# The first loads of a fused attention and gated feed-forward kernel, split over two queues, and the norm's gains loaded as rows

## The chip, the cores and the metric

The kernel runs on one core of a Trainium2 chip. The metric is device microseconds of one execution; the time of a kernel is the median of its runs. The profile is one execution of its own, recorded by the hardware profiler.

## The reference

Linear attention without a softmax, normed per head, and then a feed-forward layer with a sigmoid gate:

```python
# q, k, v: (8, 8, 576, 64) fp32; g_norm: (64,)
kv  = einsum('bhsd,bhse->bhde', k, v)
out = einsum('bhsd,bhde->bhse', q, kv)
out = out / sqrt(mean(out * out, -1) + 1e-6) * g_norm
x   = out.transpose(0, 2, 1, 3).reshape(4608, 512)
y   = (sigmoid(x @ w_gate) * (x @ w_val)) @ w_out   # w_gate, w_val: 512x1536, w_out: 1536x512
```

The weights come as 64-bit floats, 8 bytes an element, and the kernel turns them into 32-bit floats itself, with integer and float steps on VectorE and ScalarE.

## The kernel before

The rows of x are worked on in nine chunks of 512. Chunk 0 goes through both weight layers with plain products; the later chunks use a fast matrix scheme with fewer products (lines 1037 and 1139), which is most of the time and which the change does not touch. Attention of batch 0 is done in the head of the program, in four pairs of heads; attention of the later batches is fed in between the products of the chunks.

The order of the work is written out by hand: a manual schedule is used, and each engine executes its instructions in the order in which the code emits them. For the head that order is a string of tokens, `order`. `KV0`, `KVO0`, `Q0`, `QO0`, `U0`, `SQ0`, `SUM0`, `ROOT0`, `NORM0`, `X0`, `XO0` are the steps of pair 0: the product of k and v on TensorE (L346) and its copy by VectorE (L350), the turn of q by TensorE (L356) and its copy by ScalarE (L361), the output product (L373), its squares (ScalarE, L378), their sum (VectorE, L382), root (ScalarE, L386), the norm (VectorE, L390 and L392), the turn of the normed rows by TensorE (L400) and their copy to xT (ScalarE, L409). `warm10` is ten products of the identity with itself (L727), whose result nobody reads; they stand where TensorE would otherwise wait. `g0.0` to `g0.4` and `v0.0` to `v0.4` are the five steps of the conversion of a gate and a value block (L212, L230, L242, L247, L254), `ag` and `av` their steps on ScalarE (L217, L235), and `b0.0.0` and so on are products of chunk 0 (L666). The beginning reads:

```python
w1 w2 warm10 KV0 warm4 Q0 KVO0 QO0 warm3 U0 KV1 KVO1 Q1 SQ0 QO1 SUM0 ROOT0 g0.0 warm4 U1 NORM0 SQ1 ...
```

Ahead of these tokens the loads are emitted: `load_kv(n)` loads k and v of pair n (L97, 288 KB each), `load_q(n)` loads q of the pair in two halves, one for each head (L104, 144 KB each), and `load_unit(0, ...)` the gate block and then the value block of the first 64-bit weight unit (L163, 512 KB each). All of these are issued by SyncE. `g_norm` is loaded by ScalarE into `g_col`, one column of 128 partitions, in two transfers of 64 elements (L321); then ScalarE loads its table with a first square root (L325). `g_col` is read in the last conversion step of every gate and value block (L254). The identity is made by GpSimd (masks.py:197 and 199); GpSimd's queue has no transfer before the late q loads (L122).

A transfer issued by SyncE or ScalarE signals the end of its landing on one of eight semaphores, which are handed out in turn. The issue of a transfer waits until the last user of its semaphore has landed, so at most eight of these transfers are under way, and an issue that waits holds all that follows it on its engine. GpSimd's transfers have eight semaphores of their own.

Of the kernel before, what the change touches and what calls it, by code (L numbers as in the profile page):

```python
# [10 lines left out]
FP32 = mybir.dt.float32  # L11
# [10 lines left out]
def kernel(  # L22
# [11 lines left out]
    nc = tc.nc  # L34

    B, H, S, HD = q.shape
    T, DM = out.shape
    DF = moe_w_gate.shape[1]
    P = 128
    NHP = H // 2  # L40
    NJ = 6
# [10 lines left out]
    QB = 32  # L52
    NAT = 3
    NC = HD // QB
# [8 lines left out]
    NMT = DM // P  # L63
# [10 lines left out]
    RIGHT, LEFT, MIDDLE = 480, 128, 288  # L74
    const = ctx.enter_context(tc.tile_pool(name="const", bufs=1))
# [10 lines left out]


    NE = NHP
    pairs = {n: {} for n in range(B * NHP)}

    def load_kv(n):
        if n >= NE:
            return
        b, h0 = n // NHP, 2 * (n % NHP)
        for name, src in (("k", k), ("v", v)):
            t = first.tile([NP, 2, NJ * HD], FP32, tag=name, name=name)
            nc.sync.dma_start(out=t, in_=src[b, h0:h0 + 2].rearrange("h (p j) d -> p h (j d)", j=NJ))  # L97
            pairs[n][name] = t

    def load_q(n):  # L100
        h0 = 2 * n
        t = first.tile([NP, NJ, 2, HD], FP32, tag="q", name="q")
        for e in range(2):
            nc.sync.dma_start(out=t[:, :, e, :], in_=q[0, h0 + e].rearrange("(p j) d -> p j d", j=NJ))  # L104
        pairs[n]["q"] = t

    q_late = {}
# [45 lines left out]
    def load_unit(u, halves=(0, 1)):  # L153
        if u >= len(units):
            return
        kind, f = units[u]
        if 0 in halves:
            staged[u] = raw.tile([P, 2, DM], I64, tag="st", name="st", bufs=NST)
        st = staged[u]
        for i in halves:  # L160
            if kind == "gv":
                src = (moe_w_gate, moe_w_val)[i].rearrange("(m p) f -> p m f", p=P)[:, :, P * f:P * f + P]
                nc.sync.dma_start(out=st[:, i].rearrange("p (m f) -> p m f", m=NMT), in_=src)  # L163
            else:
                nc.sync.dma_start(out=st[:, i], in_=moe_w_out[P * (f + i):P * (f + i) + P, :])

# [27 lines left out]
    def convert(u):  # L194
# [42 lines left out]
        def s2(some=slice(None)):  # L237

            m = d["m"]
            if u > 2:  # L240
                load_unit(u - 1 + NST, (1,))
            vec.scalar_tensor_tensor(out=m[:, some], in0=words(u)[0][:, some], scalar=2.0 ** -52, in1=m[:, some],  # L242
                                     op0=ALU.mult, op1=ALU.add)
# [6 lines left out]
        def s4(some=slice(None)):  # L250

            m, p = d["m"][:, some], d["p"].bitcast(FP32)[:, some]
            if kind == "gv":
                vec.scalar_tensor_tensor(out=m, in0=m, scalar=g_col, in1=p, op0=ALU.mult, op1=ALU.mult)  # L254
            else:
                vec.tensor_tensor(out=m, in0=m, in1=p, op=ALU.mult)
            if u > 1 and some.stop != NMT:
                load_unit(u + NST, (0,))
# [36 lines left out]
            elif u + 1 in BY_SCALAR:  # L295
                conversion[u + 1]["ahead"][i - 2]()

    for n in range(4):
        load_kv(n)
        load_q(n)  # L300
        if n in (1, 2):
            load_unit(0, (n - 1,))


    eps = const.tile([P, 1], FP32, name="eps")
    g_col = const.tile([P, 1], FP32, name="g_col")
    unused = const.tile([P, 1], FP32, name="unused")
    const.tile([P, LEFT // 4], FP32, name="low_pad")
    w1 = const.tile([P, N3, 4 * NMT, 2, P], FP32, name="w1")
    w2 = const.tile([P, NFT, DM], FP32, name="w2")  # L310
    ident = const.tile([P, P], FP32, name="ident")
# [5 lines left out]
    qTs = const.tile([P, QW], FP32, name="qTs")  # L317
    sqs = const.tile([P, 2 * NU * P], FP32, name="sqs")
    xTs = const.tile([P, NC, 2, S // 2], FP32, name="xTs")
    for e in range(2):  # L320
        nc.scalar.dma_start(out=g_col[HD * e:HD * e + HD], in_=g_norm.rearrange("(d o) -> d o", o=1))  # L321
    make_identity(nc, ident)
    nc.vector.memset(eps, 1e-6)

    nc.scalar.activation(out=unused, in_=eps, func=AF.Sqrt)  # L325


    NX = 3
# [271 lines left out]
    def store(c, t, ot, cols=slice(0, DM), queues=(nc.sync,)):  # L600

        r0 = i = 0
        while r0 < P:
            b, s = divmod(G * c + P * t + r0, S)
            rows = out[S * b:S * b + S, cols]
            if b < NE // NHP:
                j, p = divmod(s, NP)
# [42 lines left out]
    def early(n):  # L650

        def ps(kind):
            if kind == "kv":
                return pair_kv.unsqueeze(1)
            return psum0.tile([P, 2, 512], FP32, tag="q" if kind == "q" else f"ux{n % 2}", name="two")
        return ps
# [34 lines left out]
    KV, KV_OUT, Q, Q_OUT, U, U_SQUARE, U_SUM, U_ROOT, U_NORM, X, X_OUT = range(11)  # L691
    a = [attention(n, early(n)) for n in range(NE)]

# [14 lines left out]
    for token in order.split():  # L708
        name = token.rstrip("0123456789.")
        n = [int(i) for i in token[len(name):].split(".")]  # L710
        f = n[0]
        if name == "b":
            if f not in blks:
                if f:
                    two = early(NE)("q")
                blks[f] = Plain(0, F_ORDER[f], (two[:, 0], two[:, 1]) if f else (warm, pair_kv))
            blks[f].mm(n[1], n[2])
        elif name in ("G", "E"):
            (blks[f].gate if name == "G" else blks[f].end)()
        elif name in ("g", "v", "ag", "av"):  # L720
            m0 = NMT * (name[-1] == "v")
            conversion[f]["a" if name[0] == "a" else "c"][n[1]](slice(m0, m0 + NMT))
        elif name == "w":
            load_unit(f)
        elif name in ("warm", "warmk"):
            for _ in range(f):
                nc.tensor.matmul((warm if name == "warm" else pair_kv)[:, 0:P], ident, ident, start=True, stop=True)  # L727
        else:
            a[f][steps[name]]()
            if token == f"Q{NE - 1}":  # L730
                first_ctx.__exit__(None, None, None)
                hp = ctx.enter_context(tc.tile_pool(name="hp", bufs=1))
                h_main = [hp.tile([P, 4 * NT, P], FP32, name=f"h{j}") for j in range(N3)]
                h_more = hp.tile([P, N3, 3 * NT, P], FP32, name="h_more")
# [159 lines left out]
    for some in places.split():  # L894
        p, names = some.split(":")
# [372 lines left out]
```

## Time and profile before

| | us |
|---|---|
| runs | 997.12, 997.27, 997.98; median 997.27 |
| profiled execution, its time | 996.52 |
| profiled execution, span of the trace | 994.7 |
| TensorE (PE) busy | 989.4 |
| VectorE (DVE) busy | 715.0 |
| GpSimd (POOL) busy | 614.1 |
| ScalarE (ACT) busy | 349.1 |

The span goes from the first to the last instruction in the trace; the execution's own time is 1.8 us longer. In the views, PE is TensorE's product, PEld its weight load, SPq, ACTq and POOLq are the sequencers of SyncE, ScalarE and GpSimd, whose DMA issues are not counted as busy time. A product of 32-bit floats takes several passes, so one product is two rows in the trace at most places (20 rows for ten warming products). The ends of TensorE's rows are modelled.

### The profile page before, as it was taken

Reading aid. Unit: us, or ns where it says so; the run is one execution under the profiler, and the core shown is the slowest. Engines: PE = TensorE matmul, PEld = TensorE weight load, DVE = VectorE, ACT = ScalarE, POOL = GpSimd, SP = SyncE. Lnnn points to the kernel's source line nnn. Section 1 sums busy time; section 2 is a strip of 40 time slices with the busy share of each in tenths; the row PEclk is TensorE's granted clock in tenths of the full one; section 3 lists DMA queues with packets and bytes.
Section 4 is the critical chain, followed back from the end, with each engine's and each line's share of the span. In section 5 each row is a group of like instructions: output and inputs, shape, how many; then the busy total and the mean of one; then the engine's idle time right before and its main releaser. Section 6 shows DMA issues by size and latency. Waiting matters only on the chain.

```text
span 994.7 us, 16605 instructions
## 1 busy us (share of the span) xinstructions
PE 989.4 (99%) x5958; PEld 814.9 (82%) x5958; DVE 715.0 (72%) x1199; ACT 349.1 (35%) x631; POOL 614.1 (62%) x991
## 2 busy tenths in 40 slices
PE   9999999999999999999999999999999999999998
PEld 7454448888888888888888888888888888888887
DVE  5999997898768666785777576866686566756672
ACT  5577523661244213530344124412442133213320
POOL 1349996798169625864386717870786359734963
PEclk9999999999999999999999999999999999999999
DMA  9986507662889568746975677656854455545514
GB/s 275 291 239 219 166 28 210 193 236 89 277 278 282 170 190 275 197 151 195 271 225 162 204 224 248 184 163 210 280 165 156 139 198 190 165 141 172 214 48 123
DMA packets 149523, 194.97 MB, mean 196 GB/s; under 512 B 79840, under 2 KB 121696, under 8 KB 149440
## 3 DMA queue, kind: packets, MB, share of 16 engines
q0 software_dynamic: 22512, 116.41, 35.3%
q1 hardware_dynamic: 120848, 75.66, 26.5%
q10 hardware_dynamic: 6080, 1.84, 0.8%
q8 instruction: 47, 0.77, 0.3%
q14 instruction: 36, 0.29, 0.1%
HBM read 160.04 MB, written 25.56 MB: 187 GB/s over the span
## 4 chain that ended last, share of the span: by engine, by line
PE 99%; ACT 0%; POOL 0%; issue 0%; DVE 0%; POOLq 0%; ACTq 0%
PE mm L1037 54%; PE mm L1139 27%; PE mm L666 7%; PE mm L913 4%; PE at L497 2%; PE mm L727 1%; PE at L447 1%; PE two L666 1%; PE at L666 1%; PE mm L447 1%; PE mm L346 0%; PE two L373 0%; PE two L356 0%; PE at L436 0%; PE two L400 0%; ACT qTs L361 0%
## 5 line engine op out<-in xcount | busy, mean ns | idle before, releaser
L1037 PE MATMUL mm<-xs,w 128*128 128x256 f32 x1428 | 331.3, 379 | 0.0
L1037 PEld LDWEIGHTS mm<-xs,w 128*128 128x128 f32 x1428 | 270.9, 190 | 37.0
L1037 PE MATMUL mm<-xT,w 128*128 128x256 f32 x948 | 230.5, 380 | 0.0
L1037 PEld LDWEIGHTS mm<-xT,w 128*128 128x128 f32 x948 | 179.6, 190 | 25.0 <-issue 0.5
L855 POOL DMA_DIRECT2D w<-kept x84 | 46.9, 559 | 203.1 <-PE mm L1037 199.6
L1007 DVE TENSOR_TENSOR sg<-sg,mm 128x512 f32<-128x512 f32 (+1 forms) x176 | 100.8, 600 | 89.8 <-PE mm L1037 34.3
L1139 PE MATMUL mm<-w,h 128*128 128x256 f32 x630 | 142.9, 379 | 0.0
L1139 PEld LDWEIGHTS mm<-w,h 128*128 128x128 f32 x630 | 119.6, 190 | 16.4 <-POOL h L999 0.2
L1003 ACT COPY temps<-mm 128x512 f32<-128x512 f32 (+1 forms) x128 | 66.0, 537 | 187.1 <-PE mm L1139 94.7
L999 POOL TENSOR_TENSOR h<-h,sg 128x512 f32<-128x512 f32 x72 | 96.6, 1360 | 46.0 <-ACT sg L996 30.2
L808 POOL TENSOR_TENSOR h<-h 128x128 f32<-128x128 f32 x216 | 110.5, 524 | 16.5 <-DVE h_more L808 13.1
L1139 PE MATMUL mm<-w,h_more 128*128 128x256 f32 x474 | 108.2, 379 | 0.0
L996 ACT ACTIVATE sg<-sg 128x512 f32<-128x512 f32 x96 | 59.7, 630 | 127.3 <-DVE sg L1007 127.3
L1139 PEld LDWEIGHTS mm<-w,h_more 128*128 128x128 f32 x474 | 90.1, 190 | 12.2
L1003 ACT COPY sg<-mm 128x512 f32<-128x512 f32 (+1 forms) x112 | 57.1, 510 | 87.5 <-PE mm L1139 45.3
L808 POOL TENSOR_TENSOR h_more<-h 128x128 f32<-128x128 f32 x120 | 58.6, 492 | 34.6 <-DVE h L999 30.3
L1007 DVE TENSOR_TENSOR temps<-temps,mm 128x512 f32<-128x512 f32 (+1 forms) x96 | 59.5, 620 | 26.6 <-PE mm L1139 16.9
L1007 DVE TENSOR_TENSOR temps<-mm,temps 128x512 f32<-128x512 f32 (+1 forms) x64 | 39.9, 623 | 53.3 <-PE mm L1139 23.9
L1003 ACT COPY h<-mm 128x512 f32<-128x512 f32 x48 | 28.1, 585 | 129.9 <-PE mm L1037 116.4
L666 PE MATMUL mm<-xT,w 128*128 128x512 f32 x160 | 70.1, 595 | 0.0
L1007 DVE TENSOR_TENSOR sg<-mm,sg 128x512 f32<-128x512 f32 (+1 forms) x64 | 39.7, 620 | 41.8 <-PE mm L1139 21.9
L808 POOL TENSOR_TENSOR h<-h,h_more 128x128 f32<-128x128 f32 x120 | 60.9, 508 | 4.6
(164 smaller groups left out, 1273.9 us busy)
## 6 DMA issues: line engine op xcount, KB each, us to landing
w<-kept POOLq DMA_DIRECT2D x42, 896.0 KB, 5.4
w<-kept POOLq DMA_DIRECT2D x90, 384.0 KB, 4.3
w<-kept POOLq DMA_DIRECT2D x42, 768.0 KB, 5.0
out_dram<-sg SPq DMA_DIRECT2D x119, 64.0 KB, 1.7
q<-in_q_dram SPq DMA_DIRECT2D x96, 72.0 KB, 5.0
xT<-xTs SPq DMA_DIRECT2D x96, 72.0 KB, 4.4
st<-in_moe_w_gate_dram SPq DMA_DIRECT2D x12, 512.0 KB, 6.2
st<-in_moe_w_val_dram SPq DMA_DIRECT2D x12, 512.0 KB, 6.4
```

The costliest lines, as they stand in the source:

```text
L447: nc.tensor.matmul(ps[m][HD * g:HD * g + HD, e], mains[2 * m + g, "k"][:, c], mains[2 * m + g, "v"][:, c], start=(b == 2 and e == 0 and j ...
L497: nc.tensor.matmul(to[HD * e:HD * e + HD], qTs[HD * g:HD * g + HD, c:c + HD], kvq[HD * g:HD * g + HD, m, e], start=True, stop=True)
L666: nc.tensor.matmul(self.ps[i], w[("wg", "wv")[i], self.f][:, m, :], xT[self.c][:, m, :], start=(m == 0), stop=(m == NMT - 1), skip_group_c ...
L808: ops.append((eng, lambda v=v, x=x, sign=sign, y=y, eng=eng: eng.tensor_tensor(out=h_form(v, j), in0=h_form(x, j), in1=h_form(y, j), op=op ...
L855: nc.gpsimd.dma_start(out=granule(g)[:, 0:n], in_=kept1[g // NPA % N3, g % NPA][:, 0:n])
L913: nc.tensor.matmul(ps[t], gv[0, f][:, P * t:P * t + P], w["wo", f], start=(f == 0), stop=(f == NFT - 1), skip_group_check=True)
L996: nc.scalar.activation(out=o["o" + step[1]], in_=o["o" + step[1]], func=AF.Sigmoid)
L999: mult.tensor_tensor(out=o[x], in0=o[x], in1=o[y], op=ALU.mult)
L1003: nc.scalar.copy(out=o[out_], in_=o[expr])
L1007: tt(out=o[out_], in0=o[x], in1=o[y], op=ALU.add if sign == "+" else ALU.subtract)
L1037: nc.tensor.matmul(regions[name][1][:, g], ws[:, g], xf[c][wv], start=(new and g == 0), stop=True, skip_group_check=True)
L1139: nc.tensor.matmul(regions[name][1], h_form(hv, j), ws[:, j], start=(used[i] and j == 0), stop=(j == N3 - 1), skip_group_check=True)
```

## The change

- The loads of pair 0 stay ahead of the constants; the loads of pairs 1 to 3 and the first gate and value block are emitted after them, in the same order among themselves.
- v of pairs 0, 1 and 2, the second half of q of pairs 0 and 1, and the second half of the first gate block (which becomes two transfers of 256 KB) are issued by ScalarE. On ScalarE, the first two of them stand ahead of the table load, and the other four behind the first square root.
- `g_norm` is loaded by GpSimd as four rows of 32 elements, each into the first row of a block of 32 partitions of `g_rows` (a part of `xTs` that is not yet in use, cleared by VectorE before). After the token `KVO0` VectorE turns `g_rows`, block by block of 32 by 32, into `g_turned`, whose first column is the new `g_col`.
- The string `order` is the same. The instructions of TensorE are the same in number, kind and order.

On the two queues the first transfers then stand in this order, with the landing that an issue waits for in brackets:

```
SyncE:   k0, first half of q0, k1, first half of q1, first half of the gate block, k2 [k0],
         first half of q2 [first half of q0], second half of q2 [first half of q1],
         value block [v1], k3 [first half of the gate block], v3 [second half of q1], q3 ...
ScalarE: v0, second half of q0, (table load, square root), v1, second half of q1 [v0],
         second half of the gate block [second half of q0], v2 [k1], then the copy of q of pair 0
GpSimd:  identity, four rows of g_norm
```

```diff
     def load_kv(n):
...
+            queue = nc.scalar if name == "v" and n < NTWO + 1 else nc.sync
-            nc.sync.dma_start(out=t, in_=src[b, h0:h0 + 2].rearrange("h (p j) d -> p h (j d)", j=NJ))
+            queue.dma_start(out=t, in_=src[b, h0:h0 + 2].rearrange("h (p j) d -> p h (j d)", j=NJ))
...
     def load_q(n):
...
+            queue = nc.scalar if e == 1 and n < NTWO else nc.sync
-            nc.sync.dma_start(out=t[:, :, e, :], in_=q[0, h0 + e].rearrange("(p j) d -> p j d", j=NJ))
+            queue.dma_start(out=t[:, :, e, :], in_=q[0, h0 + e].rearrange("(p j) d -> p j d", j=NJ))
...
+                if u == 0 and i == 0:
+                    for m, queue in ((0, nc.sync), (NMT // 2, nc.scalar)):
+                        queue.dma_start(out=st[:, i].rearrange("p (m f) -> p m f", m=NMT)[:, m:m + NMT // 2],
+                                        in_=src[:, m:m + NMT // 2])
+                else:
...
-    for n in range(4):
-        load_kv(n)
-        load_q(n)
-        if n in (1, 2):
-            load_unit(0, (n - 1,))
+    load_kv(0)
+    load_q(0)
...
-    g_col = const.tile([P, 1], FP32, name="g_col")
+    g_turned = const.tile([P, LEFT // 4], FP32, name="g_turned")
+    g_col = g_turned[:, 0:1]
...
-    for e in range(2):
-        nc.scalar.dma_start(out=g_col[HD * e:HD * e + HD], in_=g_norm.rearrange("(d o) -> d o", o=1))
+    g_rows = xTs[:, 0, 0, 0:QB]
+    nc.vector.memset(g_rows, 0.0)
     make_identity(nc, ident)
+    for n in range(P // QB):
+        nc.gpsimd.dma_start(out=g_rows[QB * n:QB * n + 1], in_=g_norm.rearrange("(o i d) -> o i d", o=1, d=QB)[:, n % NC])
     nc.vector.memset(eps, 1e-6)
...
     nc.scalar.activation(out=unused, in_=eps, func=AF.Sqrt)
+    for n in range(1, 4):
+        load_kv(n)
+        load_q(n)
+        if n < 3:
+            load_unit(0, (n - 1,))
...
+            if token == "KVO0":
+                nc.vector.transpose(g_turned[:, 0:QB], g_rows)
```

(`NTWO` is 2, `QB` 32, `P` 128, `NMT` 4, `NC` 2, `HD` 64.)

## The prediction

> **What bounds the kernel now.** I read the chain of waits of the first 24 us first, because every edit of the diff lies there, then the busy time by stretch, then the timelines of the queues that the edits touch. In the chain the columns are start, length, and what held the end.
>
> ```profile
> 1.02 0.30 POOL ident masks.py:199
> 1.32 0.04 issue
> 1.37 4.46 PE mm L727 x20
> 5.82 0.85 PE mm L346 x24
> 6.67 1.09 PE mm L727 x8
> 7.76 0.50 PE two L356 x6
> 8.26 0.70 PE mm L727 x6
> 8.95 0.03 issue
> 8.99 0.81 PE two L373 x40
> 9.80 0.85 PE mm L346 x24
> ...
> 21.84 0.65 ACT qTs L361
> ```
>
> The chain runs on TensorE from the moment the identity exists (1.37 us), and no DMA stands in it: L727 are the warming multiplications, L346, L356 and L373 the k-v, q and output products of a pair. TensorE by stretch says the same:
>
> ```profile
> 1.40:6.00 4.60, 4.60 (x28) 4.48 (x30) 0.00 (x0) 1.49 (x2) 0.00 (x0) 1.00 0.84 237
> 6.00:12.00 6.00, 5.97 (x122) 5.57 (x118) 1.45 (x4) 2.01 (x4) 0.00 (x0) 1.00 1.10 297
> 18.00:24.00 6.00, 5.94 (x101) 3.73 (x92) 5.56 (x13) 4.35 (x10) 1.94 (x3) 1.00 1.04 323
> ```
>
> The first number behind the comma is busy TensorE: 4.60 of 4.60, 5.97 of 6.00, 5.94 of 6.00 us; from 36 to 990 us it is busy throughout. The last two columns, DMA share and GB/s, say that the transfers already fill the DMA engines (shares near and over 1) at 237 to 323 GB/s. So the loads are busy, but TensorE does not wait for them: the warming multiplications fill the time until data land. That is what decides this case, since the change leaves TensorE's instructions and their order as they are, warming ones included.
>
> **SyncE.** The transfers below move in part to ScalarE:
>
> ```profile
> 0.74 0.38 SPq L97 DMA_DIRECT2D k<-in_k_dram  x1
> 1.18 0.44 SPq L97 DMA_DIRECT2D v<-in_v_dram  x1
> 1.66 1.40 SPq L104 DMA_DIRECT2D q<-in_q_dram  x2
> 3.10 0.62 SPq L97 DMA_DIRECT2D k<-in_k_dram  x1
> 3.76 0.45 SPq L97 DMA_DIRECT2D v<-in_v_dram  x1
> 4.26 1.24 SPq L104 DMA_DIRECT2D q<-in_q_dram  x2
> ```
>
> SyncE loses v of pairs 0 to 2 (0.44, 0.45, 0.67 us of issue), the second half of q of pairs 0 and 1 (about 0.7 and 0.63) and half a gate load. Its k of pair 1 then goes out at about 0.74 + 0.38 + 0.73 + gaps = 2.0 us instead of 3.10. What could TensorE gain? Its first k-v product waits for k and v of pair 0: v landed 3.6 us after its issue, at 4.8 us, while the product starts at 5.75, when ten warming multiplications are through. The second half of q lands 4.5 us after 2.43, at 6.9; its product starts at 7.60. Both had 0.7 to 0.9 us to spare, so earlier landings buy nothing. All that is not TensorE in the chain between 1.37 and 36 us is 0.65 (the q copy above) and some 0.15 of issue, 0.8 us together, and it waits for engines, not loads; 0.8 us is the bound of the gain, and I take 0.
>
> [...]
>
> The late loads: v of pair 3 lands at about 19.5 (issued 11.98, landing 7.6 us later, the longest of the v rows), its product starts at 20.19. After the change k of pair 3 is issued behind the landing of half a gate load (the semaphore that it shares) instead of q of pair 1. The whole gate load lands 6.2 us after 5.55, at 11.7, so k may go out up to 1.2 us later than its 10.52. At that moment k, v and q of pair 2 and the value load, 1376 KB, are still queued, 4.8 us at 290 GB/s: the engines do not run dry, and the bytes ahead of pair 3 are the same. Cost 0; if the cover failed, up to 1.2 - 0.65 = 0.6 us.
>
> **ScalarE.** It loses two g_col issues and gets six transfers: v and half a q of pair 0, then behind the table load v, half a q, half a gate load and v of pair 2. Before:
>
> ```profile
> 0.75 1.21 ACTq L321 DMA_DIRECT2D g_col<-in_g_norm_dram  x2
> 2.00 1.28 ACT L325 ACT_TABLE_LOAD   x1 [2.00 <-issue]
> 3.29 0.20 ACT L325 ACTIVATE unused<-eps 128x1 f32<-128x1 f32 x1
> 8.29 0.64 ACT L361 COPY qTs<-two 128x576 f32<-128x576 f32 x1 [4.80 <-PE two L356]
> ```
>
> The first two cost 0.44 + 0.7 = 1.1 us in place of 1.21, so the table load stays at 2.0. The last four cost about 0.45 + 0.63 + 0.62 + 0.67 = 2.4 us, under the 4.80 us that ScalarE is idle. But three of them wait for landings: half of q of pair 1 for v of pair 0, half the gate load for half of q of pair 0, and v of pair 2 for k of pair 1. Queued behind that last one is the copy of q at 8.29, and for that copy waits TensorE's output product at 8.99 (three warming multiplications fill only up to about 8.8). In the trace k of pair 1 landed 4.8 us after 3.10, at 7.9. With the same landing, v of pair 2 is issued from 7.9 to 8.6 (0.67 us) and the copy is 0.3 us late; with the longest issue of a row, 1.39 us (k of pair 2), to 9.3, 1.0 us late. But k of pair 1 is now third in its queue, issued 1.1 us earlier, with 288 KB less ahead of it on that queue: at a landing before 7.6 us nothing is late. Bounds 0 and 1.0; I take 0 to 0.3, as fewer bytes stand ahead of it.
>
> **g_norm.** Four row loads of 128 bytes go on GpSimd's queue after the identity, from 1.3 us; GpSimd is idle until 22.06, so their issue is free. VectorE clears the target (0.06 us by its memsets) and turns the rows after the k-v copy of pair 0. A turn of 128x64 takes 202 ns (L526), which bounds this 128x32 turn. It now waits for the four landings, and behind it on VectorE stand the k-v copy of pair 1, at 10.69, and the sum and norm of pair 0:
>
> ```profile
> 6.72 0.22 DVE L350 COPY kvq<-mm 128x64 f32<-128x64 f32 x1 [5.70 <-PE mm L346]
> 10.69 0.23 DVE L350 COPY kvq<-mm 128x64 f32<-128x64 f32 x1 [3.75 <-PE mm L346]
> 10.84 0.81 DVE L382 TENSOR_REDUCE ms<-sqs 128x10 f32<-128x640 f32 x1
> ```
>
> The 3.75 us of idle time is the cover. The nearest rows of GpSimd's queue:
>
> ```profile
> L122 POOL DMA_DIRECT2D h<-in_q_dram x8: 668/668/892, 22.1 to 27.0; - x8
> DMA to landing us min/median/max: 6.2/7.1/7.6
> ```
>
> With 0.89 + 2 x 0.67 the fourth is issued at about 3.6. The ScalarE g_col loads landed after 3.4 us in the median, which gives 7.0; the 7.6 above, for 72 KB each beside full engines, gives 11.2. I take some 8 to 10, nearer the GpSimd rows, since it is the same queue. The norm of pair 0 (12.45 to 13.27) has 0.8 us before its transposition on TensorE at 14.10, and the output product of pair 1 starts at 12.14 while the copy ends at 10.92: the rows may land until about 11.3 before TensorE waits. Cost 0. The wait for g_col at the conversion of 17.47 us falls away, worth 0, as it had landed by 5.
>
> Sum: 0, with up to 0.3 us more. The profiled execution took 996.52 us (span 994.7 and 1.8 around it), 0.75 under the median of the runs, 997.27 (997.12 to 997.98). On the median I forecast 997.3 us.
>
> **The rivals.** (a) ScalarE is held by v of pair 2: k of pair 1 lands after 7.6 us, the q copy and with it TensorE slip by 0.3 to 1.4 us (landing at 8.3 and the longest issue): about 998.0, no more than 998.7. For it: the wait is real and in order; against it: k is issued earlier than before. It is slower, but not by a measurable amount.
>
> (b) The slower side: g lands late on GpSimd's queue. From 11.3 us on, each microsecond holds VectorE's k-v copy of pair 1 and so TensorE. To cost over 2.0 us the fourth row must land after 13.3, 9.7 us after its issue. For it: tiny packets behind full DMA engines on a queue whose first use the trace shows only at 22 us. Against: no row landed later than 7.6 us. At a landing of 13.8 the time is 999.8.
>
> (c) The clock. The first 20 warming passes take 4.46 us, 0.223 each, the next 8 take 1.09, 0.136, and the ten at 12.95 take 1.31, 0.131: TensorE starts slow. If all 20 went at 0.131, 1.8 us would be won, and with the 0.8 above 2.6: 994.7. If TensorE stalled and a second such slow stretch came, 1.8 us and the stall would be lost. The order and start of the warming work are unchanged, so little speaks for either. [...]
>
> **How the numbers follow.** Forecast, no TensorE wait added or removed beyond 0.3 us or the 0.8 bound: 0.68. (a) 0.15, (b) 0.12, (c) 0.05. 0.2% is 2.0 us, about what a measurement of this kernel can tell from no change. Over 2.0 us slower: most of (b), 0.10, and 0.01 of (c). Faster: 0.04, the early clock of (c). The rest, 0.85, is within. The range takes in the forecast with its 0.8 us of possible gain and (a) up to 1.4 us: 996.4 to 998.7, 0.83 of the chance.
>
> **What would show it.** Right: TensorE's first product still at 5.75 us, the output product of pair 0 within 0.3 us of 8.99, the k-v copy of pair 1 within 0.2 us of 10.69, the first gate product near 18.27, the chain still without a DMA. Step by step: the table load at 2.0; the turn on VectorE before 10.7; k of pair 1 landing before 7.6. Wrong: the q copy late behind v of pair 2 (a), the turn after 11.3 with the k-v copy behind it (b), or a first warming group shorter or longer than 4.46 us by over a microsecond (c).

## The result, and the profile after

The changed kernel takes 1000.30 us (median of 8 runs, 998.67 to 1002.78), the kernel before 997.01 in the same comparison. The ratio is 1.0036, 95% interval 1.0026 to 1.0046: slower by about 3.3 us, outside the forecast range. The profiled execution took 1000.48 us (span 998.7) against 996.52 before. TensorE still executes the same instructions in the same order. Of the 4.0 us between the two profiled executions, 3.3 arise in the first 16 us and 0.6 behind TensorE's last product. From the chain of waits of the first 24 us after the change (start, length, what held the end):

```profile
1.95 7.78 DMA k<-in_k_dram
9.73 0.02 issue
9.75 0.33 ACTq L99
10.08 0.04 issue
10.12 0.65 ACT qTs L374
10.77 0.04 issue
10.81 0.81 PE two L386 x40
11.62 1.27 PE mm L359 x24
12.89 1.18 PE two L369 x6
14.07 1.54 PE mm L740 x8
```

Before, this chain ran on TensorE from 1.37 us and held no load at all. Now it begins with the load of k of pair 1, goes through ScalarE's issue of v of pair 2 (L99), which waited for it, and the copy of q of pair 0 (L374), which stood behind that issue. Only then does TensorE start the output product of pair 0 (L386), at 10.81 instead of 8.99 us. The queue of ScalarE shows the same:

```profile
1.93 1.28 ACT L333 ACT_TABLE_LOAD   x1 [1.93 <-issue]
1.99 0.57 ACTq L99 DMA_DIRECT2D v<-in_v_dram  x1
3.22 0.20 ACT L333 ACTIVATE unused<-eps 128x1 f32<-128x1 f32 x1
5.40 0.60 ACTq L107 DMA_DIRECT2D q<-in_q_dram  x1
6.04 1.17 ACTq L168 DMA_DIRECT2D st<-in_moe_w_gate_dram  x1
9.75 0.33 ACTq L99 DMA_DIRECT2D v<-in_v_dram  x1
10.12 0.64 ACT L374 COPY qTs<-two 128x576 f32<-128x576 f32 x1 [6.69 <-DMA k<-in_k_dram]
```

v of pair 1 (second row) is issued while the table load runs, not behind it. The copy of q comes after 6.69 us of idle time that ended with the landing of k. The second loss is the clock. TensorE by stretch, cut where the clock changes (busy TensorE stands first behind the length, the granted clock third from the end):

```profile
5.01:8.43 3.42, 3.42 (x48) 3.23 (x48) 0.23 (x1) 0.00 (x0) 0.00 (x0) 1.00 0.97 257
8.43:11.84 3.41, 1.32 (x52) 1.06 (x52) 0.21 (x1) 0.79 (x2) 0.00 (x0) 1.00 1.16 266
11.84:15.26 3.42, 3.42 (x35) 3.27 (x32) 1.62 (x5) 1.40 (x3) 0.00 (x0) 0.50 1.15 269
15.26:18.67 3.41, 3.41 (x70) 3.10 (x71) 2.17 (x4) 1.93 (x4) 0.00 (x0) 1.00 1.11 263
```

In the second stretch TensorE is busy for 1.32 of 3.41 us; in the third it is busy throughout, but at a granted clock of 0.50. The sum of the loss: the output product of pair 0 is 1.82 us late (2.09 us of idle time, less 0.27 since the work ahead of it was through earlier in this execution), the half clock adds 1.5 us, and from 15.6 us to the last product the shift stays at 3.3 to 3.4.

The third loss is at the end. VectorE's last operation, before and after:

```profile
990.85 0.42 DVE sg L1007
```

```profile
994.19 0.42 DVE sg L1022
```

From its start to the end of the span it is 3.88 us before and 4.52 after, though the last stores are issued by 1.3 us after that start in both. So the span is 4.0 us longer.

The rows of `g_norm` did what was forecast. On VectorE:

```profile
6.48 0.23 DVE L363 COPY kvq<-mm 128x64 f32<-128x64 f32 x1 [5.43 <-PE mm L359]
9.29 0.21 DVE L744 STREAM_TRANSPOSE g_turned<-xTs 128x32 f32<-128x32 f32 x1 [2.58 <-DMA xTs<-in_g_norm_dram]
12.94 0.23 DVE L363 COPY kvq<-mm 128x64 f32<-128x64 f32 x1 [3.44 <-PE mm L359]
```

The four rows landed at 5.9 to 9.16 us; the turn took 0.21 us at 9.29, ahead of the k-v copy of pair 1, which waited for TensorE.

### The profile page after: what moved, and what is told of

It reads as the page before. It is cut to its first block, busy times and chain, and to the rows that moved or that the text cites. A ratio compares the mean times of both kernels' runs of the same rounds, so it can differ in the third digit from the quotient of the medians.

```text
span 998.7 us, 16615 instructions
## 1 busy us (share of the span) xinstructions
PE 990.6 (99%) x5958; PEld 817.3 (82%) x5958; DVE 715.0 (72%) x1201; ACT 349.0 (35%) x631; POOL 614.7 (62%) x995
## 4 chain that ended last, share of the span: by engine, by line
PE 98%; DMA 1%; SPq 0%; ACT 0%; DVE 0%; issue 0%; ACTq 0%
PE mm L1052 54%; PE mm L1154 27%; PE mm L679 7%; PE mm L928 4%; PE at L510 2%; DMA k<-in_k_dram 1%; PE at L460 1%; PE two L679 1%; PE at L679 1%; PE mm L460 1%; PE mm L740 0%; PE two L386 0%; PE mm L359 0%; PE two L413 0%; PE two L369 0%; PE at L449 0%
```

## The experiments

Line numbers differ by a few from kernel to kernel: the output product is `two<-kvq,qTs`, the q product `two<-ident,q`, the copy of q `qTs<-two`.

**The theory** after the result had three parts. The hold: v of pair 2 waits on ScalarE for k of pair 1 and holds the copy of q. The order: the second half of q of pair 1 waits to be issued (for the landing of v of pair 0, at 5.40 us), and half the gate block and k of pair 2, which SyncE issues meanwhile, go ahead of it; it landed at 12.79 instead of 9.93. The clock: TensorE's idle time (2.09 us) is followed by a stretch at half clock (11.84 to 15.26). **The rivals**: the rows of `g_norm`; two queues that make all loads late; something outside the head.

**e1: the hold removed.**

```diff
-            queue = nc.scalar if name == "v" and n < NTWO + 1 else nc.sync
+            queue = nc.scalar if name == "v" and n < NTWO else nc.sync
```

> The changed kernel with one edit: v of pair 2 is issued by SyncE again. Theory (the hold): ScalarE's issue of v of pair 2 waits for the landing of k of pair 1 (9.73 us) and holds the copy of q of pair 0, so TensorE stalls 2.1 us at the output product, and the stall costs a 3.4 us stretch at half clock, 1.3 us more. Without it the copy starts at about 8.1 us, the output product at 8.8, no half-clock stretch, and the time is that of the kernel before within 0.5 us (996.5 to 997.5). Rival 1 (two queues slow the loads): k and v of pair 1 land at 9.7 in any case, and TensorE waits at the k-v product of pair 1 instead: at 0.1 to 0.5 us late the time is up to 997.5, and should pair 1 or 2 land later still, 998 to 1000. Rival 2 (g_norm on GpSimd's queue): it stays in this kernel, so the time stays at 1000.3.

Measured: 1002.9 us (1000.73 to 1004.36), ratio 1.0056 (1.0042 to 1.0070). The hold is gone and nothing is won. The chain of waits of e1:

```profile
9.55 0.81 PE two L386 x40
10.37 0.87 PE mm L359 x24
11.24 1.53 issue
12.77 0.69 PE two L369 x6
```

The output product starts at 9.55, but the q product of pair 1 stands until 12.77: the second half of its q landed at 12.68. (The view calls the 1.53 us issue and names no releaser.) At 13.66 a half-clock stretch begins. So the hold is not the only wait: a second one, the order, stands right behind it.

**e2: the hold covered by more warming work.**

```diff
-... QO0 warm3 U0 ...
+... QO0 warm12 U0 ...
```

> The changed kernel with twelve warming products ahead of the output product of pair 0 instead of three, so that TensorE works through the 2.1 us in which it waited; the q copy is as late as before. Theory (the stall also costs the clock): the output product starts at 10.8 as in the changed kernel, but no half-clock stretch follows, so from there on all is 1.3 us earlier than in the changed kernel: 999.0, and the runs scatter less than 998.7 to 1002.8. Rival (the half-clock stretch has another cause, or costs nothing): 1000.3.

Measured: 1005.4 us (1003.14 to 1005.81), ratio 1.0071 (1.0057 to 1.0084). In the head the clock part held: the output product came at 11.29 with no idle time and no half clock between 6.44 and 716 us, and pair 3's output product was 2.3 us late instead of 3.4. But two stalls in the middle of the kernel, which no other trace has in that size, outweighed it. The chains around them:

```profile
499.04 1.28 issue
```

```profile
712.41 2.54 issue
```

TensorE waits for nothing that the profile shows; the second is followed by a half-clock stretch from 716.42 to 719.83. The longer program shifts all that follows it, so this run says nothing clean about the time, and the cause of these stalls stays open.

**e3 and e4: one half of the change each.** e3 is the kernel before with the rows of `g_norm` and the turn; e4 is the change with `g_col` loaded by ScalarE as before.

```diff
 e4:
-    for n in range(P // QB):
...
+    for e in range(2):
+        nc.scalar.dma_start(out=g_col[HD * e:HD * e + HD], in_=g_norm.rearrange("(d o) -> d o", o=1))
```

> The kernel before with g_norm alone changed: four rows on GpSimd's queue, turned by VectorE behind the first k-v copy; all other loads on SyncE. The hold: nothing waits on ScalarE, so 997.0 within 0.5 us, the q copy at 8.3 us and k of pair 1 landing near 7.9. Rival 2 (the g rows are what slows k of pair 1, or VectorE is held by them): k of pair 1 lands by 1 us or more later, and part of the 3.3 us shows, 998 or more.

> The changed kernel with g_norm loaded as before by ScalarE (two transfers behind the second half of q of pair 0); the k, v, q and gate loads are split over the two queues. With the two extra transfers the semaphores go round otherwise: on ScalarE the second half of the gate block now waits for k of pair 1, and v of pair 2 for the first half of q of pair 1, which lands after k of pair 1. The hold: the q copy starts behind that landing, at 10 to 11.5 us, and the time is 1000 to 1002. Rival 2 (g on GpSimd's queue is the cause): 997. Rival 1 (two queues slow the loads, hold or not): k of pair 1 lands near 9.7 again without any g row.

Measured: e3 997.32 us, ratio 1.0002 (0.9993 to 1.0011), so the rows by themselves cost nothing. e4 997.9 us, ratio 1.0009 (1.0000 to 1.0017): nearly nothing either, and a miss of the expectation. The reason is the turn of the semaphores. The two `g_col` transfers of ScalarE take two of the eight, so v of pair 1 now waits for the landing of k of pair 0 and goes out at 4.80, well behind k of pair 1 (1.95); k then lands at 7.14 instead of 9.73. v of pair 2 waits for a landing at 7.82, and the copy of q is not held. The second half of q of pair 1 lands at 11.08, for 0.27 us of idle TensorE. The split over two queues is the same; who waits for whom, and which bytes travel side by side, is not.

**e5, e6, e12: q of pair 1 issued in time.** In e5 the square root with its table load stands behind the loads of pair 1 on ScalarE, so that this half of q has a semaphore of the first turn; v of pair 2 stays on ScalarE and waits for v of pair 1. e6 is e5 with the edit of e1. In e12 the half of q goes to SyncE, which also makes v of pair 2 wait for k of pair 0 only.

```diff
 e5:
-    nc.scalar.activation(out=unused, in_=eps, func=AF.Sqrt)
     for n in range(1, 4):
         load_kv(n)
         load_q(n)
+        if n == 1:
+            nc.scalar.activation(out=unused, in_=eps, func=AF.Sqrt)
 e12:
-            queue = nc.scalar if e == 1 and n < NTWO else nc.sync
+            queue = nc.scalar if e == 1 and n < 1 else nc.sync
```

> The square root with its table load stands behind v and q of pair 1 on ScalarE, so the second half of q of pair 1 goes out in the first turn of the semaphores, without a wait; v of pair 2 stays on ScalarE and now waits for the landing of v of pair 1. The hold alone. My theory (two waits, each enough): v of pair 1 lands at 9 to 10 us, the copy of q of pair 0 is held until about 9.5 to 10.3, the output product of pair 0 starts at 10.2 to 11.0 after 1.4 to 2.3 us of idle TensorE, a half-clock stretch of about 3.4 us follows, the q product of pair 1 does not wait for its load; time 999.5 to 1000.5. Rival 1 (the order of the loads alone is the cause, the hold only a name in front of it): the output product slips, but the rest catches up, 997 to 998. Rival 2 (the rows of g_norm or another edit): unchanged at 1000.3 with no idle TensorE before the output product.

> As the run before, and v of pair 2 is issued by SyncE: neither the hold nor the late q, with the split of all other loads and the rows of g_norm kept. My theory: output product of pair 0 at 9.0 to 9.3, q product of pair 1 without a wait of over 0.3 us, no half-clock stretch after 6 us, time 996.5 to 997.7. Rival 1 (more bytes under way at once make every load late, however issued): k or v of pair 1 lands after 10.5 and TensorE waits for it, 998.5 to 1000.5. Rival 2 (something outside the head, or the rows of g_norm): 1000 as after the change.

> The changed kernel with one edit: the second half of q of pair 1 is issued by SyncE, behind the first half. It then has a semaphore of the first turn and waits for nothing, and v of pair 2 on ScalarE comes to wait for the landing of k of pair 0 instead of k of pair 1. Everything else stays split. My theory (the two waits are the loss): copy of q of pair 0 at 8.5 to 9.1 us, no idle time over 0.4 us before 14 us, no half-clock stretch, 997 to 998.5. Rival (two queues share the transfers, so that all land late): k or v of pair 1 lands after 10.3 us and TensorE waits for it, 999 or more.

Measured: e5 998.32 us (997.02 to 998.91 and one run of 1003.29), ratio 1.0014 (1.0004 to 1.0025); e6 998.24, ratio 1.0007 (0.9999 to 1.0016); e12 998.41, ratio 1.0013 (1.0004 to 1.0021). By the medians some 60 to 65% of the loss is gone in all three, and no trace has a half-clock stretch in the head. In e5 I had expected the hold to show, but v of pair 1 landed at 8.38 in its trace and the copy of q was nearly in time:

```profile
1.93 6.45 DMA v<-in_v_dram
...
8.78 0.65 ACT qTs L375
```

e6 issues the same first eight transfers, and there the same v landed at 9.62 and k at 9.88 instead of 8.76: landings scatter by over a microsecond between executions. The time of e6 missed its expectation (997.7 at most).

What is left is some 1.2 us by the medians. In the three traces 0.75 to 1.0 us of the loss stands behind TensorE's last product (see e9, below). In the head short waits are left: 0.25 us for the copy of q in e5, and in e6 a third wait, 0.65 us at 15.66. There TensorE needs the normed rows of pair 0, and ahead of their norm VectorE had waited for the second half of the gate block, which landed at 14.01 (the whole block landed at 11.70 before). In e12 the q product of pair 0 was late for the first time, because the first half of its q, which was under way together with k and v of pair 1, landed at 8.66 (before: 5.47). TensorE's timeline:

```profile
8.79 0.69 PE L369 MATMUL two<-ident,q 96*128 96x96 f32 x6 [0.86 <-DMA q<-in_q_dram]
```

Another 0.4 to 0.7 us in e6, e12 and e7 (below) is a wait for a copy of ScalarE near 714 us, which I did not pursue.

**e7: only pair 0 split.** v and the second half of q of pair 0 on ScalarE, all later loads on SyncE in the old order, `g_norm` as rows.

```diff
-            queue = nc.scalar if name == "v" and n < NTWO + 1 else nc.sync
+            queue = nc.scalar if name == "v" and n < 1 else nc.sync
-            queue = nc.scalar if e == 1 and n < NTWO else nc.sync
+            queue = nc.scalar if e == 1 and n < 1 else nc.sync
-                if u == 0 and i == 0:
+                if False:
```

> Only v and the second half of q of pair 0 are issued by ScalarE, all later loads by SyncE in the order of before, the gate block whole; g_norm as rows on GpSimd's queue as in the change. My theory: k of pair 1 lands before 7.6 us, as no v is issued beside it, nothing holds ScalarE, landings of pair 1 within 0.7 us of before, TensorE without a wait, 996.5 to 997.5. Rival 1 (the rows of g_norm beside the split make k of pair 1 late): k of pair 1 after 8.5 us, though TensorE may not notice. Rival 2 (earlier loads help): under 996.

Measured: 997.53 us, ratio 1.0004 (0.9996 to 1.0013), no idle TensorE in the head. k of pair 1 landed at 8.05, where I had expected under 7.6; it was not late enough to matter. The split of pair 0 and the rows of `g_norm` together cost TensorE nothing in the head when no v travels beside k of pair 1 and nothing waits on ScalarE.

**e8, e10, e11: a hold by itself.** The kernel before, its loads and TensorE's program unchanged, with squares on ScalarE that nobody reads ahead of the copy of q: 24, 20 and 17 of them.

```diff
+    for _ in range(24):
+        nc.scalar.activation(out=sqs[:, 0:P], in_=ident, func=AF.Square)
```

> The kernel before, with 24 squares of the identity on ScalarE ahead of the copy of q of pair 0, whose results nobody reads; loads and TensorE's program as before. It asks what a hold costs by itself. My theory: at 0.2 to 0.27 us each the copy is held until 9 to 10.5 us, TensorE idles by 0.8 to 2.4 us before the output product of pair 0; when it idles by over 1.5 us a half-clock stretch of about 3.4 us follows and costs 1.2 to 1.7 us more, so the time is the idle time + 1.5 above before, 999.5 to 1001. Rival 1 (the clock fell for another reason in the change): the idle time alone, 998 to 999.4. Rival 2 (the idle time is given back by later stretches in which TensorE waits anyway): 997 to 997.7.

> As the hold of 24 squares, with 20, to end at the same place as in the changed kernel: at 0.341 us each the copy of q of pair 0 begins at about 10.2 us, TensorE idles by 1.5 to 2.3 us. Loads as before. My theory: the idle time, and a half-clock stretch of one period (+1.2 to 1.7 us) if most of the idle time falls in one period: 999 to 1001. Rival (the late q of pair 1 alone made the clock fall in the change): no half-clock stretch, 998.5 to 999.3.

> The same hold with 17 squares: the copy of q of pair 0 begins at about 9.2 us, TensorE idles by 0.5 to 1.3 us. My theory: so short a stall leaves the clock as it is, since 0.65 us did, so only the idle time is lost: 997.5 to 998.5, granted clock 1.0 after the first rise. Rival (any stall costs a period of half clock): 999 to 1000.

Measured: 24 squares 1001.99 us, ratio 1.0045 (1.0032 to 1.0059); 20 squares 999.85, ratio 1.0029 (1.0018 to 1.0040); 17 squares 997.25, ratio 1.0005 (0.9997 to 1.0014). The squares followed each other every 0.34 us where I had guessed 0.2 to 0.27 for the first of these kernels, so its hold was longer than planned, 3.73 us of idle TensorE. With 20 the copy of q begins at 10.08, nearly as in the changed kernel (10.12), and TensorE idles for 2.33 us. TensorE by stretch, with 20 squares:

```profile
7.81:11.23 3.42, 1.09 (x38) 0.90 (x40) 0.00 (x0) 2.69 (x8) 0.00 (x0) 1.00 1.06 305
11.23:14.64 3.41, 3.41 (x56) 3.17 (x48) 1.28 (x3) 0.93 (x2) 0.00 (x0) 0.50 1.17 248
14.64:18.05 3.41, 3.41 (x51) 3.07 (x50) 1.04 (x2) 1.19 (x3) 0.00 (x0) 0.50 1.11 241
18.05:21.50 3.45, 3.45 (x50) 3.26 (x50) 2.98 (x7) 2.51 (x8) 0.00 (x0) 1.00 1.14 290
```

No load was moved, and the same picture comes: a stretch with 1.09 of 3.42 us busy, then half clock, here twice as long. By the medians this hold costs 2.8 us, against 3.3 for the change. The trace is one of the two slowest of its six runs (1001.26). In it the output product comes 1.76 us later than before (2.33 of idle time, less 0.57 since the clock rose at 4.40 instead of 5.51) and the last product 4.76 later, so the half clock, 6.83 us of it, cost 3.0 us, 1.5 for each 3.413 us as in the change. With 17 squares, where I had expected 0.5 to 1.3 us of idle time, TensorE did not wait for the copy at all in the trace, that of the slowest run (999.22): the clock rose late, at 7.35, and TensorE was later with it; a stall of 1.04 us at 16.57 left the clock at full.

**e9, e13, e14: the changed kernel, unaltered, three more traces.**

> The changed kernel once more, unaltered, for a second trace of it. So far every half-clock stretch in the traces has lasted 3.413 us or twice that, and the time from the first rise of the clock to its fall is 2, 208 or 290 times 3.413 us, as if the clock were decided once per period of a grid that starts where it will. My theory (the idle time of the two late loads, and the clock falls for the next period when a period holds much of it): a rise anywhere between 4.3 and 7.3 us, a fall a whole number of periods later, 1.0 to 2.3 us of idle time before the output product of pair 0 or the q product of pair 1, time 998.5 to 1002.8. Rival (the clock falls a fixed time after a stall): the fall is not a whole number of 3.413 us after the rise.

> The changed kernel, a third trace. My theory (landings decide): time above 997.0 = the idle time of TensorE before 14 us + about 1.5 us for each half-clock period behind a period less than two thirds busy, to within 0.7 us; k of pair 1 after 9.3 us goes with 999.5 or more, before 8.8 with 998.5 or less. Rival (the loss is elsewhere, after the head): the shift of TensorE's rows against before at 30 us is under half of the shift at the end.

> The changed kernel, a fourth trace; expectations as for the third.

Measured: e9 999.38 us median (997.91 to 1002.77, 12 runs), ratio 1.0025 (1.0015 to 1.0034). The four traces of this one kernel, by the landing of k of pair 1 (times in us; the last column is how much later than before TensorE's last product starts):

| trace | time | k of pair 1 lands | idle before the output product, and before the q product of pair 1 | half clock | TensorE's shift |
|---|---|---|---|---|---|
| e9 | 997.91 | 8.43 | 0.38, 0 | none | 0.66 |
| e14 | 998.45 | 8.90 | 1.05, 0.21 | none | 1.33 |
| the first | 1000.48 | 9.73 | 2.09, 0 | 3.413 | 3.34 |
| e13 | 1002.16 | 9.72 | 1.84, 0.20 | 6.827 | 5.02 |

The copy of q begins 0.39 us after k's landing in all four. The chains of waits of e9 and of e13:

```profile
1.96 6.47 DMA k<-in_k_dram
8.43 0.02 issue
8.45 0.33 ACTq L99
8.78 0.04 issue
8.82 0.65 ACT qTs L374
9.46 0.04 issue
9.51 0.81 PE two L386 x40
```

```profile
1.95 7.76 DMA k<-in_k_dram
9.72 0.02 issue
9.74 0.33 ACTq L99
10.06 0.04 issue
10.11 0.65 ACT qTs L374
```

So the chain is the same each time, and the landing sets its length. With the same landing the first trace and e13 lie 1.7 us apart, as one has 3.413 us at half clock and the other 6.827. Taking the idle time, 1.5 us for each 3.413 us of half clock and 997.0 for the kernel before, the four times come out as 997.4, 998.3, 1000.6 and 1002.0, within 0.6 us of the measured ones, as e13's expectation had said. All but 0.1 us of each of TensorE's shifts is there by 20 us, so of these the rival outside the head falls.

It does not fall for the end. The rule of sum starts from the median 997.0, 0.5 us above the trace of before (996.52), and this hides that each of the four also ends later behind TensorE: 4.49 to 4.59 us from the start of VectorE's last operation to the end of the span, 3.88 before. From 996.52, the shift of the last product and this longer end together give each of the four times to 0.02 us. The kernels that keep the old loads (before, e3, e8, e10, e11) have 3.87 to 3.96 us there, and all thirteen traces with loads on two queues have 4.30 to 4.88, e4 (4.47) and e7 (4.30) among them. So 0.4 to 1.0 us goes with the split, whatever happens in the head: 0.6 in e4 and 0.4 in e7, whose medians lie 0.9 and 0.4 us above before. No run asked which part of the split does it.

**e15, e16: e1 again, two more traces.**

> v of pair 2 on SyncE, a second trace. My theory: the q product of pair 1 waits 1 to 2 us for its late second half, landing at 12 to 13 us, and one or two half-clock periods follow (1.5 us each); the run's time is accounted for within 0.7 us by 30 us. Rival (a stall in mid-kernel, as with the longer warming): over 1.5 us of the loss lie after 100 us.

> v of pair 2 on SyncE, a third trace; expectations as for the second.

Measured: 999.09 and 1000.44 us. The q product of pair 1 idled for 0.55 and 1.65 us behind landings of its second half at 12.29 and 12.10; half clock followed the longer stall only (12.13 to 15.54). In e15 the q product of pair 0 waited 0.66 us more for a landing at 8.62. (The four single traces e13 to e16 were taken beside one run of the kernel before, 997.69.) So e1 loses by the late q of pair 1, each time. By the rule of sum above e16 comes to 1000.2, but e15 to 998.2, 0.9 short, which misses the 0.7 of its expectation. The rule leaves out the end, which is 0.86 us longer in e15 than before, and the clock, which rose at 6.32 and made the head itself later. Why e1's five timed runs (1002.9) lay above these two is not settled; the four above 1000.73 have no trace.

## Why the prediction was wrong

**The step that failed first is ScalarE's, at the landing of k of pair 1.** The prediction put it before 7.6 us, because k "is now third in its queue, issued 1.1 us earlier, with 288 KB less ahead of it on that queue". The issue did come 1.1 us earlier (1.95), but the landing came at 9.73, 8.43, 9.72 and 8.90 in the four traces, later than the 7.93 of before. So the hold, which the sum took at 0 to 0.3 us, made the output product 1.82 us late in the first trace (0.5 to 1.8 in the other three), and where the stall was long it brought the clock's 1.5 us, which the sum did not have.

What counted here was not only what is ahead on its own queue. v of pair 1 was issued from the other queue at 1.99 us, 0.04 behind k, so that 1440 KB were issued up to the two instead of 1152, and in e5, e6, e9 and e12 to e16 k and v of pair 1, issued 0.02 to 0.04 us apart, landed 0.3 to 1.1 us apart. In the kernels that issue v behind k (e3, e4, e7, e8, e10, e11) k landed at 7.14 to 8.05; in all that issue the two side by side, at 8.43 to 10.04. A better bound was the landing of v of pair 1, the end of 1440 KB in the old order: 8.24, 8.61 and 8.80 in e3, e8 and e11, where the old loads stand. Even this is too early for three of the four landings: when k landed at 9.73, about 2.0 MB had moved (210 GB/s from the start), so bytes of transfers issued behind it had moved by then too. One more slip fed this: I placed v of pair 1 "behind the table load", but ScalarE issued it during that load.

**The order of q of pair 1 had no price in the sum.** It was issued 0.53 us later (5.40, 4.87 before) and landed 2.86 us later, with 2272 KB issued up to it instead of 1728. The prediction listed its wait for v of pair 0, but did not ask who is issued meanwhile. This alone costs TensorE 0.55 to 1.65 us as soon as the hold is away (e1, e15, e16), so the two waits lie side by side, and taking only the first one away wins nothing.

**Rival (a) named the mechanism and mis-sized it.** Held by v of pair 2, decided by k's landing: that is what the chain shows. Its price was capped at 1.4 us with a landing at 8.3; the landing was up to 9.73 and the idle time 2.09. Its issue, bounded by 0.67 to 1.39 us, took only 0.33.

**Rival (c) held the other half of the price, and was not joined to (a).** "If TensorE stalled and a second such slow stretch came, 1.8 us and the stall would be lost" is what happened, at 1.5 us for one stretch and 3.0 for two. I had given the slower side of it 0.01, since the warming order is unchanged; but the stall that starts it is rival (a)'s own.

**What held:** nothing is gained from earlier loads (e7: 0.4 us, within the interval of no change); the rows and the turn of `g_norm` cost nothing (e3), the turn came before 10.7, so rival (b) was wrong; the late loads of pair 3 (k landed at 20.65 instead of 18.53) held nothing up; the table load came at 1.93, for 2.0 before.

**What the prediction did not look at** is the end of the span, where 0.4 to 1.0 us are lost in every trace with split loads, and the second half of the gate block, whose wait it listed without a price and which held TensorE by 0.65 us in e6.

**What stays open:** why the span ends later behind TensorE with split loads; why the same transfers land up to 1.3 us apart between executions of one kernel, and whether the hold on v of pair 1, as in e5, often costs anything; one of e5's 11 runs, 1003.29, lies apart and has no trace.

## What to carry to other kernels

When loads are spread over two queues, write them down in one list in the order of issue, with the landing that each issue waits for: here a k of 288 KB landed at 8.43 to 10.04 us with a v issued beside it on the other queue and at 7.14 to 8.05 without, and a load that waited for a semaphore, the second half of q of pair 1, was overtaken by what the other queue issued meanwhile and landed at 12.79 instead of 9.93. A transfer that waits must not stand ahead of work that a busy engine needs soon: here v of pair 2 held the copy of q until 10.12, for 8.29 before. A stall of TensorE is to be priced together with the granted clock: here 1.6 to 2.3 us of idle time went with a loss of some 3 to 5 us, while no half clock followed stalls of 0.4 to 1.3 us. The end of the span belongs to the comparison too, not only the stretch that was edited.

## What the runs showed of the hardware

In the clock records of the 18 traces the time from the first rise to the next fall was 6.827 us in six, 709.97 in e2, and 989.865, to the end of the work, in the rest: 2, 208 and 290 times 3.413 us. Each half-clock stretch between a fall and the next rise lasted 3.413 or 6.827 us. The first rise came anywhere between 4.31 (e8) and 7.35 us (e11), with the first product always at 1.36 or 1.37, and TensorE's head moved with it: where it did not wait, the q product of pair 0 began between 7.03 (e8) and 8.40 us (e11).

In these traces the clock fell behind stretches of 3.41 us in which TensorE was busy for 0.67 (e8) to 1.85 us (e1), and stayed behind those with 2.13 (e2, at 499 us) or more. The two sides, e16 and then e14, TensorE by stretch:

```profile
8.71:12.13 3.42, 1.80 (x66) 1.45 (x64) 1.16 (x3) 0.83 (x2) 0.00 (x0) 1.00 1.14 280
12.13:15.54 3.41, 3.35 (x30) 3.15 (x34) 1.47 (x3) 0.84 (x2) 0.00 (x0) 0.50 1.17 297
```

```profile
8.89:12.31 3.42, 2.17 (x71) 1.94 (x71) 0.83 (x3) 1.34 (x2) 0.00 (x0) 1.00 1.16 302
12.31:15.72 3.41, 3.41 (x65) 3.22 (x64) 2.52 (x5) 2.15 (x4) 0.00 (x0) 1.00 1.12 315
```

How long the half clock then lasted did not go by the busy time: after 1.09 us (20 squares) it was 6.827 us, after 1.32 (the first trace of the change) 3.413, after 1.57 (e13) 6.827.
